# Opening loads, first-chunk normalisation, group-load timing and final-store queue of a one-core attention + gMLP kernel

## The chip, the cores and the metric

The kernel runs on one core of a Trainium2 chip. The metric is device time in microseconds (us) of one execution. Before the change the median of four runs is 1329.87 us (1329.43 to 1330.57).

A core has five engines that run their own instruction streams in order: TensorE (PE in the profile, with PEld for its weight loads), VectorE (DVE), ScalarE (ACT), GpSimd (POOL) and SyncE (SP). DMA transfers are issued by SP, ACT or POOL as instructions of their streams, so a DMA waits behind whatever its issuer is still waiting for; the transfer itself runs beside the engines. Matrix products land in PSUM banks; operands lie in SBUF.

## The reference, cut to what matters

One block with adaptive layer norms: a modulation vector from `c`, grouped-query attention (32 query heads, 8 key/value groups, 2048 tokens, 2048 cached keys, head size 128), and a gated MLP whose spatial product mixes tokens.

```python
mod = (silu(c) @ w_mod).reshape(1, 6, 1, 512)
sa, ca, ga, sb, cb, gb = mod[:, 0..5]
h = layernorm(x) * (1 + ca) + sa                    # x: 1 x 2048 x 512
q = h @ wq                                          # 32 heads of 128
o = softmax(q @ k_cache.T * 128**-0.5) @ v_cache    # 4 query heads per k/v group
x = x + ga * (o @ wo)
h = layernorm(x) * (1 + cb) + sb
z = gelu(h @ w_in);  z1, z2 = halves of z;  z2 = layernorm(z2)
x = x + gb * ((z1 * (w_sp @ z2 + b_sp)) @ w_out)
```

## The kernel before

Tokens are 16 tiles of 128 rows, taken in four chunks of four tiles (CT = 4). The attention runs as 128 units: unit `it` is group `it // 16`, token tile `it % 16`, all four query heads of the group. A unit has eight slots. In a slot, `qk` (L914) makes two score matmuls of 128 keys by 512 columns (4 heads x 128 rows) into a two-bank PSUM tile, and ACT takes the exponential of 1024 columns; `pv` (L936) makes eight matmuls of the previous unit's probabilities by the values, with normalisation by VectorE after every half of a unit (`rall`, `onorm`, L955 and L956), and after slot 7 a DMA transpose of the result (`oT`, L964, on SP). Three units later `wo_proj` (L968) multiplies by `wo`.

The order of all instructions is written out by hand. `at(it, slot, fn)` puts a piece of work ahead of the slot's score matmuls; `fill[it, slot]` lists matmuls that come after them. The loop at L1202 emits slot by slot; each engine keeps the order in which its instructions were emitted. `qproj(b, ...)` (L873) projects the queries of block b (one group, one chunk) as fill matmuls, with a copy of each PSUM bank to SBUF by VectorE (`qT`, L894).

Layer norm of a chunk has three pieces: `ln1_stats` (L796: two VectorE instructions per tile, then two small ones on POOL for the reciprocal root, `rstd_of` L669), `ln1_norm` (L801: one VectorE pass per tile), and the turn to columns with scale and shift. For chunk 0 and 1 the turn is on TensorE, `ln1_turn` (L824), through the two PSUM banks called `misc`, with `ln1_mod` (L814) out of PSUM by VectorE, or in part by ACT; for chunks 2 and 3 it is by DMA transposes on SP (`ln1_dma`, L852) and in-place `ln1_mod` passes (L857). The `misc` banks also hold the modulation columns, the query projections and the `wo` products.

The opening is issued on SP in this order: `c`, row tile 0 of x, the first third of `w_mod` (L698, columns for shift and scale), half the keys of group 0 in natural order, `wq` of group 0, row tiles 1 to 3 of x (L735), the other keys by DMA transpose, values, the rest of x, `wo`. TensorE fills the time with `warm(n)` matmuls on zeros (L762), then `mod_columns` (L774) makes the shift and scale columns; row tile 0 is normalised, turned and projected, and unit 0 begins. Row tiles 1 to 3 are normalised together (L904), turned at slot 4 of unit 0, and projected in slots 5 to 7.

Group g's keys (SP transpose), values, `wo` and `wq` (POOL queue) are loaded by four entries at L1109 to L1114. The rest of `w_mod` and `w_in` come on POOL at units 2 and 5.

After the attention, the second layer norm, `w_in` products with gelu (`z2`, `z1`), and the spatial product run (`spatial`, L1274, `gb` L1294); `finish_tile` (L1308) scales, adds the residual (`yout`, two buffers) and stores a row tile. Between the first and second quarter of the spatial product SP issues 16 transposing loads of the last quarter of `w_sp` (L1340 to L1342, `load_wsp` L1055).

Of the kernel before, what the change touches and what calls it, by code (L numbers as in the profile page):

```python
# [15 lines left out]
P = 128  # L16
# [559 lines left out]
def kernel(  # L576
# [19 lines left out]
    nc = tc.nc  # L596
    _, S, D = A_x.shape
    _, HKV, SK, DH = A_k_cache.shape
    HQ = A_wq.shape[1] // DH
    REP = HQ // HKV  # L600
# [4 lines left out]
    NT = S // P  # L605
# [4 lines left out]
    CT = 512 // P  # L610
# [7 lines left out]
    x_dram = A_x[0].rearrange("(t p) d -> p t d", p=P)  # L618
    out_dram = out[0].rearrange("(t p) d -> p t d", p=P)
# [6 lines left out]
    wmod_dram = w_mod.rearrange("(p dt) n -> p dt n", p=P)  # L626
    c_dram = c[0].rearrange("(p j) -> p j", p=P)
# [18 lines left out]
    x_sb = res.tile([P, NT, D], BF16, name="x_sb")  # L646
# [9 lines left out]
    wmod_a = res.tile([P, NDT, 2 * D], BF16, name="wmod_a")  # L656
# [6 lines left out]
    def bank(name):  # L663
        return psum.tile([P, 512], FP32, name=name)
# [28 lines left out]


    c_bf = res.tile([P, NDT], BF16, name="c_bf")
    nc.sync.dma_start(out=c_bf[:], in_=c_dram)
    nc.sync.dma_start(out=x_sb[:, 0, :], in_=x_dram[:, 0, :])
    nc.sync.dma_start(out=wmod_a[:], in_=wmod_dram[:, :, 0 : 2 * D])  # L698
    k_nat = early.tile([P, SK], BF16, name="kT")
    nc.sync.dma_start(out=k_nat[:, 0:HK].rearrange("p (t d) -> p t d", d=DH), in_=k_rows)  # L700

    groups, wqs, hTs, qTs = {}, {}, {}, {}

    def load_wq(g, engine):
        wqs[g] = early.tile([P, NDT, REP * DH], BF16, name="wq_g")
        engine.dma_start(
            out=wqs[g][:], in_=wq_dram[:, :, g * REP * DH : (g + 1) * REP * DH]
        )

    def load_v(g):  # L710
        v1 = late.tile([P, NKT, DV], BF16, name="v1")
        nc.gpsimd.memset(v1[:, :, DH:DV], 1.0)  # L712
        if g > 0:
            nc.gpsimd.dma_start(out=v1[:, :, 0:DH], in_=v_dram[:, g])
        else:
            nc.sync.dma_start(out=v1[:, 0 : NKT // 2, 0:DH], in_=v_rows)
            nc.sync.dma_start(
                out=v1[:, NKT // 2 : NKT, 0:DH], in_=v_dram[:, 0, NKT // 2 : NKT]
            )
        groups[g]["v1"] = v1  # L720

    def load_wo(g, engine):
        wo_g = late.tile([P, REP, D], BF16, name="wo_g")
        engine.dma_start(out=wo_g[:], in_=wo_dram[:, g * REP : (g + 1) * REP, :])
        groups[g]["wo"] = wo_g

    def load_k(g):
        kT = early.tile([P, SK], BF16, name="kT")
        nc.sync.dma_start_transpose(out=kT[:], in_=A_k_cache[0, g])
        groups[g] = dict(kT=kT)  # L730
# [31 lines left out]
    def warm(n):  # L762

        w_ps = bank("o_ps")
        for k in range(n):
            nc.tensor.matmul(
                w_ps[:].rearrange("p (r d) -> p r d", r=REP),
                lhsT=zeros[:, 0, :],
                rhs=zeros[:],
                start=True,  # L770
                stop=True,
            )
# [23 lines left out]
    def ln1_stats(j0, n):  # L796
        for j in range(j0, j0 + n):
            ln_stats(mv1, j, x_sb[:, j, :])
        return rstd_of(mv1[:, j0 : j0 + n, :], n, "ln1")

    def ln1_norm(j0, n, rstd):  # L801
        xns = []
        for j in range(j0, j0 + n):
            xn = res.tile([P, D], BF16, name="xn1", bufs=4)
            normalise(xn[:], x_sb[:, j, :], mv1[:, j, 0:1], rstd[:, j - j0 : j - j0 + 1])
            xns.append(xn)
        return xns

    def hT_of(ch):
        if ch not in hTs:  # L810
            hTs[ch] = res.tile([P, NDT, 512], BF16, name="hT", bufs=NCH)
        return hTs[ch]
# [11 lines left out]
    def ln1_turn(j0, n, xns, on_act=()):  # L824

        ch, c0 = j0 // CT, (j0 % CT) * P
        hT = hT_of(ch)
        for half in range(2):
            t_ps = bank("misc")[:].bitcast(BF16).rearrange("p (k q) -> p k q", k=2)
            for k in range(2):  # L830
                dt = half * 2 + k
                for jj in range(n):
                    nc.tensor.transpose(  # L833
                        t_ps[:, k, jj * P : (jj + 1) * P],
                        xns[jj][:, dt * P : (dt + 1) * P],
                        ident[:],
                    )
            for k in range(2):
                dt = half * 2 + k
                dst, src = hT[:, dt, c0 : c0 + n * P], t_ps[:, k, 0 : n * P]  # L840
                if dt in on_act:
                    nc.scalar.activation(
                        out=dst,
                        in_=src,
                        func=ACT.Identity,
                        scale=modc[:, NDT + dt : NDT + dt + 1],
                        bias=modc[:, dt : dt + 1],
                    )
                else:
                    ln1_mod(dst, src, dt)  # L850
# [7 lines left out]
        for dt in range(NDT):  # L858
            ln1_mod(hTs[ch][:, dt, :], hTs[ch][:, dt, :], dt)

    warm(18)
    xns0 = ln1_norm(0, 1, ln1_stats(0, 1))
    mod_columns(0, wmod_a, 0)
    ln1_turn(0, 1, xns0, on_act=(1, 3))
# [3 lines left out]
            k_ps[:, kt * P : (kt + 1) * P], k_nat[:, kt * P : (kt + 1) * P], ident[:]  # L868
        )
    nc.scalar.copy(out=kT0[:, 0:HK], in_=k_ps)  # L870
    warm(3)

    def qproj(b, heads, c0, n):  # L873

        g, ch = divmod(b, NCH)
        if b not in qTs:
            qTs[b] = early.tile([P, REP, 512], BF16, name="qT")
        one = n * len(heads) <= 512
        ps = {}

        def mm(hh, dt):
            if dt == 0 and (not one or hh == heads[0]):
                ps[0] = bank("misc")
            o0 = (hh - heads[0]) * n if one else 0
            nc.tensor.matmul(  # L885
                ps[0][:, o0 : o0 + n],
                lhsT=wqs[g][:, dt, hh * DH : (hh + 1) * DH],
                rhs=hTs[ch][:, dt, c0 : c0 + n],
                start=(dt == 0),
                stop=(dt == NDT - 1),  # L890
            )
            if dt == NDT - 1 and (not one or hh == heads[-1]):
                hs = heads if one else [hh]
                nc.vector.tensor_copy(  # L894
                    out=qTs[b][:, hs[0] : hs[-1] + 1, c0 : c0 + n],
                    in_=ps[0][:, 0 : len(hs) * n].rearrange("p (h q) -> p h q", q=n),
                )

        return [lambda hh=hh, dt=dt: mm(hh, dt) for hh in heads for dt in range(NDT)]

    for fn in qproj(0, list(range(REP)), 0, P):
        fn()
    rest0 = {}
    rest0["xn"] = ln1_norm(1, CT - 1, ln1_stats(1, CT - 1))  # L904


    NU = HKV * NT
# [3 lines left out]
    def at(it, slot, fn):  # L911
        later.setdefault((it, slot), []).append(fn)
# [148 lines left out]
    wsp = [None] * NCH  # L1061

    fill = {}
    rest_q = qproj(0, list(range(REP)), P, 512 - P)
    at(0, 4, lambda: ln1_turn(1, CT - 1, rest0["xn"]))
    for k, fn in enumerate(rest_q):
        fill.setdefault((0, 5 + k // 6), []).append(fn)
    for i in range(4):
        fill[0, i] = [lambda: warm(1)]

    def ln1_at(ch, stats, norm, turn):
        st = {}
        at(*stats, lambda: st.update(r=ln1_stats(ch * CT, CT)))
        at(*norm, lambda: st.update(x=ln1_norm(ch * CT, CT, st["r"])))
        if ch == 1:
            at(*turn, lambda: ln1_turn(ch * CT, CT, st["x"]))
        else:
            at(norm[0], norm[1] + 1, lambda: ln1_dma(ch * CT, CT, st["x"]))
            at(*turn, lambda: ln1_dma_mod(ch))

    ln1_at(1, (1, 0), (1, 5), (1, 7))
    ln1_at(2, (2, 4), (3, 1), (4, 5))
    ln1_at(3, (5, 1), (5, 5), (6, 6))
    rest_w = {}
    at(2, 5, lambda: nc.gpsimd.dma_start(out=wmod_b, in_=wmod_dram[:, :, 2 * D : NMOD]))
    at(5, 5, lambda: nc.gpsimd.dma_start(out=win_sb[:], in_=win_dram))
# [20 lines left out]
    for st in range(NT):  # L1107
        at(21 + 6 * st, 2, lambda st=st: load_wsp(wsp[0], 0, st))
    for g in range(1, HKV):  # L1109
        it = (g - 1) * NT + 4  # L1110
        at(it, 3, lambda g=g: load_k(g))
        at(it + 1, 3, lambda g=g: load_v(g))
        at(it + 2, 3, lambda g=g: load_wo(g, nc.gpsimd))
        at(it + 3, 3, lambda g=g: load_wq(g, nc.gpsimd))  # L1114


    zs = {}
# [127 lines left out]
    for f in range(NFT):  # L1245
# [6 lines left out]
        out=ok1[:], in0=rall[:], scalar1=1.0 / SAFE, scalar2=None, op0=ALU.is_ge  # L1252
# [8 lines left out]
        out=bad[:], in0=okm[:], scalar1=-1.0, scalar2=1.0, op0=ALU.mult, op1=ALU.add  # L1261
# [46 lines left out]
    def finish_tile(t, jj, src, parts=1):  # L1308
        j = t * CT + jj
        tmp = mlp.tile([P, D], FP32, name="tmp", bufs=2)  # L1310
        yout = mlp.tile([P, D], BF16, name="yout", bufs=2)
        w = D // parts
        for k in range(parts):
            s = slice(k * w, (k + 1) * w)
            nc.vector.tensor_tensor(out=tmp[:, s], in0=src[:, s], in1=gb_rows[:, s], op=ALU.mult)
            nc.vector.tensor_tensor(out=yout[:, s], in0=tmp[:, s], in1=x_sb[:, j, s], op=ALU.add)
            (nc.sync, nc.scalar)[k].dma_start(out=out_dram[:, j, s], in_=yout[:, s])

    yTs = {}

# [81 lines left out]
```

## Time and profile before

| what | value |
|---|---|
| median of runs | 1329.87 us |
| profiled execution | 1329.66 us |
| its span, first to last instruction | 1327.8 us |
| TensorE busy | 1314.4 us (99%) |
| ACT busy | 1078.0 us (81%) |
| VectorE busy | 473.2 us (36%) |
| first score matmul | 11.76 us |
| last unit's score matmuls end, last matmul of the kernel | about 1138 and 1321 us |
| granted TensorE clock, mean | 0.999 |

In a row of the timeline the first number is the start in us from the span's start, the second the duration (of merged rows: of the whole stretch), then the engine, the line of the kernel, the operation, output and inputs, count, and in brackets how long the engine stood idle before it and what released it. `SPq` and `ACTq` are DMA issues in those engines' streams; the duration is that of the issue, not of the transfer. In the waits view a row gives who waited for whom, and the total in us, the number of times and the longest.

### The profile page before, as it was taken

The numbers are of one execution on the slowest core, as the hardware profiler recorded it, in microseconds if no ns is written. First come the engines' busy times: TensorE is split into PE (matmuls) and PEld (weight loads), VectorE is DVE, ScalarE is ACT, GpSimd is POOL, SyncE is SP. The second block draws the span as 40 slices with busy tenths as digits, with TensorE's granted clock in tenths as the row PEclk, the third lists the DMA queues.
The fourth block names the chain that finished last, engine by engine and source line by source line (L and its number), as shares of the span: only waits on it lengthen the run. The fifth ranks groups of instructions, "written<-read, shape, count | busy, mean of one in ns | idle before, by whom it ended". The sixth has DMA issues, their size and how long they took to land.

```text
span 1327.8 us, 27856 instructions
## 1 busy us (share of the span) xinstructions
PE 1314.4 (99%) x12337; PEld 858.7 (65%) x12337; DVE 473.2 (36%) x1163; ACT 1078.0 (81%) x1060; POOL 48.5 (4%) x90
## 2 busy tenths in 40 slices
PE   8999999999999999999999999999999999999998
PEld 5666666666666666666666666666666666644445
DVE  5632222222222222222222222222222566793444
ACT  6888999999999999999999999999999999650000
POOL 1200000000000000000000000000000000120000
PEclk9999999999999999999999999999999999999999
DMA  5541031003201131013100410122101111153300
GB/s 160 118 129 13 17 70 31 17 17 67 35 17 21 33 69 21 13 37 68 18 18 17 84 21 15 21 65 36 21 13 21 25 34 33 29 119 80 64 21 27
DMA packets 145983, 57.58 MB, mean 43 GB/s; under 512 B 136160, under 2 KB 141408, under 8 KB 145856
## 3 DMA queue, kind: packets, MB, share of 16 engines
q1 hardware_dynamic: 141504, 39.29, 15.6%
q0 software_dynamic: 4208, 16.39, 4.4%
q8 instruction: 98, 1.61, 0.5%
q14 instruction: 29, 0.24, 0.1%
q10 hardware_dynamic: 144, 0.07, 0.0%
HBM read 21.37 MB, written 2.10 MB: 18 GB/s over the span
## 4 chain that ended last, share of the span: by engine, by line
PE 96%; SPq 2%; DMA 1%; DVE 1%; issue 0%; POOL 0%; DVEq 0%
PE o_ps L944 35%; PE s_ps L922 33%; PE misc L976 8%; PE misc L885 8%; PE misc L1279 6%; PE s_ps L1125 2%; PE s_ps L1164 2%; SPq L1056 1%; PE o_ps L1300 1%; PE s_ps L1300 1%; DMA wmod_a<-in_w_mod_dram 0%; DMA hT<-xn 0%; DMA out_dram<-yout 0%; PE misc L833 0%; DVE qT L894 0%
## 5 line engine op out<-in xcount | busy, mean ns | idle before, releaser
L929 ACT ACTIVATE pT<-s_ps 128x1024 bf16<-128x1024 f32 x1024 | 1044.5, 1025 | 86.9 <-PE s_ps L922 13.0
L944 PEld LDWEIGHTS <-pT 128*128 128x128 bf16 x8192 | 548.5, 98 | 242.4 <-issue 1.3
L944 PE MATMUL o_ps<-v,pT 128*128 128x129 bf16 x8192 | 631.4, 220 | 1.0 <-DVE onorm L956 1.0
L922 PE MATMUL s_ps<-qT,kT 128*128 128x512 bf16 x2048 | 608.9, 379 | 1.8 <-DVE qT L894 1.4
L955 DVE RECIPROCAL rall<-o_ps 128x2 f32<-128x2 f32 x256 | 43.7, 171 | 737.7 <-PE o_ps L944 737.4
L922 PEld LDWEIGHTS <-kT 128*128 128x128 bf16 x2048 | 199.2, 98 | 121.4 <-issue 1.7
L976 PE MATMUL misc<-wo_g,oT 128*128 128x512 bf16 x512 | 194.0, 379 | 0.0
L885 PE MATMUL misc<-hT,wq_g 128*128 128x512 bf16 (+2 forms) x528 | 190.3, 373 | 0.0
L956 DVE TENSOR_TENSOR onorm<-o_ps,rall 128x256 bf16<-128x256 f32 x256 | 108.6, 424 | 9.0 <-DVE rall L955 0.3
L1279 PE MATMUL misc<-wsp,z 128*128 128x512 bf16 (+2 forms) x560 | 100.7, 336 | 1.5 <-DVE gb L1294 1.5
L894 DVE CAST qT<-misc 128x512 bf16<-128x512 f32 (+1 forms) x129 | 87.3, 677 | 6.7 <-PE misc L885 6.6
L1279 PEld LDWEIGHTS <-z 128*128 128x128 bf16 x560 | 50.7, 98 | 50.0 <-issue 1.5
L989 DVE TENSOR_TENSOR xacc<-misc,xacc 128x512 f32<-128x512 f32 x112 | 76.2, 680 | 0.0
L885 PEld LDWEIGHTS <-wq_g 128*128 128x128 bf16 x528 | 50.6, 98 | 1.8 <-issue 0.3
L976 PEld LDWEIGHTS <-oT 128*128 128x128 bf16 x512 | 50.1, 98 | 0.7
L1294 DVE TENSOR_TENSOR gb<-misc,bsp_bc 128x512 bf16<-128x512 f32 (+1 forms) x28 | 18.4, 658 | 53.2 <-PE misc L1279 53.2
L712 POOL MEMSET v<- 128x128 bf16 x8 | 1.6, 203 | 707.9 <-issue 606.9
L1125 PE MATMUL s_ps<-win_sb,hT 128*128 128x448 bf16 x128 | 27.0, 352 | 0.0
L1135 ACT ACTIVATE z<-s_ps 128x896 bf16<-128x896 f32 x16 | 14.7, 917 | 14.9 <-PE s_ps L1125 14.9
L1164 PE MATMUL s_ps<-hT,win_sb 128*128 128x512 bf16 x112 | 24.5, 379 | 0.0
L1172 ACT ACTIVATE z1T<-s_ps 128x1024 bf16<-128x1024 f32 x14 | 14.3, 1024 | 10.1 <-PE s_ps L1164 9.1
L691 DVE BATCH_NORM_STATS2 bnst<-x_sb 128x6 f32<-128x512 bf16 x32 | 21.8, 681 | 0.5
(78 smaller groups left out, 285.3 us busy)
## 6 DMA issues: line engine op xcount, KB each, us to landing
v<-in_A_v_cache_dram POOLq DMA_DIRECT2D x7, 512.0 KB, 7.1
wo_g<-in_A_wo_dram POOLq DMA_DIRECT2D x7, 512.0 KB, 4.7
wq_g<-in_A_wq_dram POOLq DMA_DIRECT2D x7, 512.0 KB, 5.9
oT<-onorm SPq DMA_TRANSPOSE x128, 2.4
wsp<-in_w_mod_dram POOLq DMA_DIRECT2D x1, 2048.0 KB, 10.1
out_dram<-yout SPq DMA_DIRECT2D x15, 128.0 KB, 1.7
win_sb<-in_B_w_in_dram POOLq DMA_DIRECT2D x1, 1792.0 KB, 10.5
x_sb<-in_A_x_dram SPq DMA_DIRECT2D x3, 512.0 KB, 6.3
```

Source lines behind the costliest of these rows:

```text
L885: nc.tensor.matmul(ps[0][:, o0 : o0 + n], lhsT=wqs[g][:, dt, hh * DH : (hh + 1) * DH], rhs=hTs[ch][:, dt, c0 : c0 + n], start=(dt == 0), s ...
L894: nc.vector.tensor_copy(out=qTs[b][:, hs[0] : hs[-1] + 1, c0 : c0 + n], in_=ps[0][:, 0 : len(hs) * n].rearrange("p (h q) -> p h q", q=n),)
L922: nc.tensor.matmul(s_ps[:, h * 512 : (h + 1) * 512].rearrange("p (r q) -> p r q", r=REP), lhsT=groups[g]["kT"][:, kt * P : (kt + 1) * P], ...
L929: nc.scalar.activation(out=pTs[u][:, 2 * i : 2 * i + 2, :], in_=s_ps[:].rearrange("p (k q) -> p k q", k=2), func=ACT.Exp, scale=inv_sqrt_dh,)
L944: nc.tensor.matmul(o_ps[:, hh % 2, 0 : DH + 1], lhsT=pTs[u][:, kt, hh * P : (hh + 1) * P], rhs=groups[g]["v1"][:, kt, 0 : DH + 1], start=( ...
L955: nc.vector.reciprocal(out=rall[:, c0 : c0 + 2], in_=o_ps[:, :, DH])
L956: nc.vector.tensor_tensor(out=onorms[u][:, hh - 1 : hh + 1, :], in0=o_ps[:, :, 0:DH], in1=rall[:, c0 : c0 + 2].unsqueeze(2).to_broadcast([ ...
L976: nc.tensor.matmul(X_ps[:], lhsT=oTs[u][:, hh, :], rhs=groups[g]["wo"][:, hh, :], start=(hh == 0), stop=(hh == REP - 1),)
L989: nc.vector.tensor_tensor(out=xaccs[j][:], in0=X_ps[:], in1=xaccs[j][:], op=ALU.add)
L1125: nc.tensor.matmul(ps[0][:, hf * 512 : hf * 512 + FC], lhsT=h2Ts[j // CT][:, dt, (j % CT) * P : (j % CT + 1) * P], rhs=win_sb[:, dt, FH + ...
L1164: nc.tensor.matmul(ps[0][:, k * 512 : (k + 1) * 512], lhsT=win_sb[:, dt, f * P : (f + 1) * P], rhs=h2Ts[2 * ch2 + k][:, dt, :], start=(dt ...
L1279: nc.tensor.matmul(g_ps[:, :n], lhsT=z2[:, st, f * P : (f + 1) * P], rhs=wsp[t][:, st, c0 : c0 + n], start=(st == 0), stop=(st == NT - 1 a ...
```

## The change

Five edits:

1. `c` and row tile 0 are issued on ACT's queue; SP starts with `w_mod`, in two loads of 512 columns each.
2. The warm-up matmuls go from 18 and 3 to 14 and 2, and those in unit 0 from four to two.
3. Row tiles 1 to 3 of chunk 0 are handled in two steps, row tile 1 and then 2 and 3. The statistics of tile 1 are emitted before the first query projection, its turn at unit 0 slot 1, its projection (128 columns of all heads) in slot 3; tiles 2 and 3 are turned at slot 4 and projected (256 columns, two heads per bank) in slots 6, 7 and slot 0 of unit 1. The first projection's copy is shared by VectorE and ACT.
4. Chunk 1's statistics move from unit 1 slot 0 to slot 1; chunk 3's scale and shift from unit 6 slot 6 to unit 7 slot 4. The loads of each next group move from units 4 to 7 of the group's sixteen to units 7 to 9.
5. `finish_tile` stores on ACT's queue (the second half of the last tile on SP).

```diff
-    nc.sync.dma_start(out=c_bf[:], in_=c_dram)
-    nc.sync.dma_start(out=x_sb[:, 0, :], in_=x_dram[:, 0, :])
-    nc.sync.dma_start(out=wmod_a[:], in_=wmod_dram[:, :, 0 : 2 * D])
+    nc.scalar.dma_start(out=c_bf[:], in_=c_dram)
+    nc.scalar.dma_start(out=x_sb[:, 0, :], in_=x_dram[:, 0, :])
+    for i in range(2):
+        part = slice(i * D, (i + 1) * D)
+        nc.sync.dma_start(out=wmod_a[:, :, part], in_=wmod_dram[:, :, part])
...
-    warm(18)
+    warm(14)
...
-    warm(3)
-
-    def qproj(b, heads, c0, n):
+    warm(2)
+    first = {}
+    first["r1"] = ln1_stats(1, 1)
+
+    def qproj(b, heads, c0, n, two_engines=False):
...
-                nc.vector.tensor_copy(
-                    out=qTs[b][:, hs[0] : hs[-1] + 1, c0 : c0 + n],
-                    in_=ps[0][:, 0 : len(hs) * n].rearrange("p (h q) -> p h q", q=n),
-                )
+                dst = qTs[b][:, hs[0] : hs[-1] + 1, c0 : c0 + n]
+                src = ps[0][:, 0 : len(hs) * n].rearrange("p (h q) -> p h q", q=n)
+                cut = len(hs) // 2 if two_engines else len(hs)
+                nc.vector.tensor_copy(out=dst[:, 0:cut], in_=src[:, 0:cut])
+                if two_engines:
+                    nc.scalar.copy(out=dst[:, cut:], in_=src[:, cut:])
...
-    for fn in qproj(0, list(range(REP)), 0, P):
+    for fn in qproj(0, list(range(REP)), 0, P, two_engines=True):
         fn()
-    rest0 = {}
-    rest0["xn"] = ln1_norm(1, CT - 1, ln1_stats(1, CT - 1))
+    first["x1"] = ln1_norm(1, 1, first["r1"])
+    first["r2"] = ln1_stats(2, 2)
...
-    rest_q = qproj(0, list(range(REP)), P, 512 - P)
-    at(0, 4, lambda: ln1_turn(1, CT - 1, rest0["xn"]))
-    for k, fn in enumerate(rest_q):
-        fill.setdefault((0, 5 + k // 6), []).append(fn)
-    for i in range(4):
-        fill[0, i] = [lambda: warm(1)]
+    def first_turn():
+        ln1_turn(1, 1, first["x1"])
+        first["x2"] = ln1_norm(2, 2, first["r2"])
+
+    at(0, 1, first_turn)
+    at(0, 4, lambda: ln1_turn(2, 2, first["x2"]))
+    fill[0, 0] = [lambda: warm(1)]
+    fill[0, 2] = [lambda: warm(1)]
+    fill[0, 3] = qproj(0, list(range(REP)), P, P)
+    rest_q = qproj(0, [0, 1], 2 * P, 2 * P) + qproj(0, [2, 3], 2 * P, 2 * P)
+    fill[0, 6], fill[0, 7], fill[1, 0] = rest_q[0:4], rest_q[4:10], rest_q[10:16]
...
-    ln1_at(1, (1, 0), (1, 5), (1, 7))
+    ln1_at(1, (1, 1), (1, 5), (1, 7))
     ln1_at(2, (2, 4), (3, 1), (4, 5))
-    ln1_at(3, (5, 1), (5, 5), (6, 6))
+    ln1_at(3, (5, 1), (5, 5), (7, 4))
...
-        it = (g - 1) * NT + 4
-        at(it, 3, lambda g=g: load_k(g))
-        at(it + 1, 3, lambda g=g: load_v(g))
-        at(it + 2, 3, lambda g=g: load_wo(g, nc.gpsimd))
-        at(it + 3, 3, lambda g=g: load_wq(g, nc.gpsimd))
+        it = (g - 1) * NT
+        at(it + 7, 6, lambda g=g: load_k(g))
+        at(it + 8, 3, lambda g=g: load_v(g))
+        at(it + 9, 3, lambda g=g: load_wo(g, nc.gpsimd))
+        at(it + 7, 3, lambda g=g: load_wq(g, nc.gpsimd))
...
-            (nc.sync, nc.scalar)[k].dma_start(out=out_dram[:, j, s], in_=yout[:, s])
+            (nc.scalar, nc.sync)[k].dma_start(out=out_dram[:, j, s], in_=yout[:, s])
```

## The prediction

> **What bounds the kernel now.** I read the page first, then the waits of TensorE, then the timeline of the three places where TensorE waits.
>
> ```profile
> PE 1314.4 (99%) x12337; PEld 858.7 (65%) x12337; DVE 473.2 (36%) x1163; ACT 1078.0 (81%) x1060; POOL 48.5 (4%) x90
> ```
>
> TensorE is busy for 99% of the span. Any time it does not stand idle is already useful work, so a change that removes no useful matmul can only win or lose at its few stalls. Two rows of the timeline tell how regular the middle is: the first score matmuls of units 16 and 17 start at 158.57 and 167.38, 8.81 us apart. The loads of group 2 onwards, at either place, fall into such stretches. The waits of TensorE name the stalls:
>
> ```profile
> PE misc L1279 <- DVE gb L1294: 1.5, 1, 1.5
> ...
> PE o_ps L944 <- DVE onorm L956: 1.0, 1, 1.0
> ```
>
> The 1.5 is near the end (1244 us), the 1.0 at 80 us; the six others (4.1 us together) lie in the first 23 us. The timeline of the opening (columns: start, duration, engine, line, operation):
>
> ```profile
> 1.64 0.69 SPq L698 DMA_DIRECT2D wmod_a<-in_w_mod_dram  x1
> ...
> 3.50 0.82 SPq L735 DMA_DIRECT2D x_sb<-in_A_x_dram  x1
> ...
> 11.02 0.69 DVE L894 CAST qT<-misc 128x512 bf16<-128x512 f32 x1 [1.64 <-PE misc L885]
> ...
> 22.47 0.60 PE L922 MATMUL s_ps<-qT,kT 128*128 128x512 bf16 x2 [0.65 <-DVE qT L894]
> ...
> 27.09 1.38 DVE L680 TENSOR_SCALAR xn<-x_sb,mv,rstd_ln 128x512 bf16<-128x512 bf16 x4 [0.24 <-POOL rstd_ln L676]
> ```
>
> The last of these rows is a deadline: chunk 1's normalised rows are complete at 28.47 (27.09 + 1.38), and the timeline has TensorE's transposes of them start at 28.68, with 0.2 us to spare. Chunk 1's statistics had begun at 22.33, as soon as VectorE was through with the last copy of unit 0's queries. Then the two later stalls:
>
> ```profile
> 79.50 1.38 DVE L815 TENSOR_SCALAR hT<-hT,modc 128x512 bf16<-128x512 bf16 x4 [7.24 <-DMA hT<-xn]
> ...
> 81.48 0.61 PE L944 MATMUL o_ps<-v,pT 128*128 128x129 bf16 x8 [1.02 <-DVE onorm L956]
> ...
> 1220.65 21.41 SPq L1056 DMA_TRANSPOSE wsp<-in_B_w_sp_dram  x16
> ...
> 1242.16 5.47 SPq L1317 DMA_DIRECT2D out_dram<-yout  x4
> ...
> 1244.18 0.69 DVE L1316 TENSOR_TENSOR yout<-tmp,x_sb 128x512 bf16<-128x512 f32 x1 [7.94 <-DMA out_dram<-yout]
> ...
> 1245.53 10.52 PE L1279 MATMUL misc<-wsp,z 128*128 128x512 bf16 x48 [1.50 <-DVE gb L1294]
> ```
>
> At 80 us VectorE sits for 7.24 us on chunk 3's DMA transposes, and everything queued behind it starves TensorE. At 1242 us four stores leave SP only when its 16 weight transposes are issued.
>
> **Final stores on ACT's queue.** VectorE's third output tile needs one of two yout buffers; the first store is issued at 1242.16 although its tile was ready at 1227.04. On ACT's queue nothing stands ahead (its last gelu ends at 1197.5), so that store goes out about 15 us earlier; median landing is 1.7 us and tiles come 4.96 us apart. VectorE's 7.94 us wait and TensorE's 1.50 go; next late is nothing, since 0.69 + 0.69 of output work fits in 4.96. Gain 1.5. Were the stores slowed by the 16 transposes beside them, a buffer is free for two tiles, 9.9 us, so only a landing above that brings a stall back. At the very end the halves of the last tile change queues: SP's half landed in 2.4 us, ACT's in 1.9, so the last store costs between -0.2 and +0.5 us; I take 0, because the issues (0.33 and 0.38) are nearly equal.
>
> **Loads and chunk 3 later.** Chunk 3's scale-and-shift moves from unit 6, slot 6 to unit 7, slot 4. Unit 7 lasts 10.13 us (75.46 to 85.59) where 8.81 is the pitch with the same matmuls: the stall costs 1.32. The new place is TensorE's 79.86, and the transposes landed by 79.50 even with 3.3 MB of group loads beside them; with k, v, wo and wq of group 1 moved to units 7 to 9 only win (1.8 MB) shares their stretch, so they land sooner. Chunk 3's queries are projected from unit 8; four passes of 0.41 us end in time. Gain 1.32, bounds 1.0 and 1.32. What is moved: per group one SP transposing load (issue 2.48, ahead of SP's oT transposes, whose results are wanted 1.5 units, 13 us, later) and three POOL issues of 0.75 to 1.23 on an engine 4% busy. They arrive 4 or more units before use. Cost 0; without that cover, the 2.48 on SP.
>
> **Opening loads.** SP issues w_mod at 0.73 instead of 1.64, 0.91 earlier. Two parts read 1 KB rows where one load read 2 KB: by the windows view the DMA moves 392 GB/s in 6 to 7 us (2 KB rows) and 372 in 8 to 9 (1 KB), so 1 MB costs 0.15 more. The 128 KB row tile, sent ahead before, now rides beside w_mod: 0 to 0.35 at 372 GB/s. The DMA is full from 4 to 10.7 us, so all that follows comes 0.4 to 0.75 earlier; I take 0.6. Rows 1-3 of x landed at 10.70 (3.50 plus 7.2), now 10.1; wq at 9.6, now 9.0.
> The Trainium skill, DMA: Bandwidth & Descriptors, section Issuing engines are not separate DMA queues, says that DMAs started by different engines share the same 16 DMA engines and that a second queue saves only the starter's issue time. By it alone x would land 0.91 earlier and the total below would be 0.3 us lower; the sum stays with the rows.
> The new c and x issues on ACT come either ahead of the activation-table load (0.73, 1.28 us) or behind it, 1.28 later. Row 0 would then be normalised at about 7.3 instead of 6.0; both are hidden, because the first projection waits for wq until 9.0 and VectorE for x until 10.1. Price 0 either way. Seven warm-up matmuls fewer (25 to 18) free 7 x 0.216 = 1.5 us of TensorE that lay in waits: 0.
>
> **Two-step normalisation.** Here I follow VectorE's order. Behind row 0's scale-and-shift it now holds the statistics of row 1, and these wait for x at 10.1: two instructions, 0.90 us (11.62 to 12.52), end 11.0. The query copy is behind them, halved: rows give 0.69 for 512 columns and 0.56 for 384, so 0.43 for 256, end 11.4; ACT's half is long done. First scores at 11.45, before 11.76: 0.3 won. Row 1: POOL chain 1.02 (4.56 to 5.58), so normalised 12.0 to 12.4. Rows 2's and 3's statistics: 1.7, to 14.1. Row 1's four scale-and-shifts: 4 x 0.31, to 15.3. Rows 2-3 normalised 2 x 0.38, to 16.05. TensorE meanwhile does the projection of slot 3, which waits for 15.3: 13 matmuls of 0.066 more, to 16.2; its copy (0.69) ends at 16.95. The second half of the next transposes needs that PSUM bank (misc has two), so slot 4's scores start at 17.3, before 17.13. The early win is gone. From there ACT leads: exponentials every 0.92, slot 7's scores at 19.9, six matmuls, unit 1 at 20.95 (before 22.47), its second fill of six ends at 22.5, where slot 1 starts; before 23.36. That is 0.9 won.
> But chunk 1's statistics moved behind the copy of that second fill: 22.5 + 0.69 = 23.2, before 22.33. Statistics 3.28, POOL chain 1.48 (25.61 to 27.09), normalising 1.38: complete at 29.3. TensorE arrives for the transposes 5.32 after slot 1 (as 23.36 to 28.68), at 27.8; twelve of 16 need the last row, so they end at 30.05, before 29.57. The head loses 0.5. Bounds: 0.9 won if the statistics chain does not bind, 1.3 lost if x lands at 10.7 as now and 0.2 more slips.
>
> **Sum.** -1.5 - 1.32 + 0.5 = -2.3 us on the profiled execution, which took 1329.66 us (span 1327.8 plus 1.9 around it), 0.2 under the median 1329.87. From the median: 1327.6. A measurement of this kernel can tell about 0.2%, 2.7 us; this lies just inside.
>
> **Rivals.**
> The chain of chunk 1 does not bind: some 1.5 us shorter (x rows earlier, shorter copies, or statistics running between other work). For it: VectorE had 1.64 us idle before 11.02 and 0.24 at 27.09. Against: its order is fixed and POOL's 1.48 stands in it. Then the head wins 0.9: 1329.87 - 3.7 = 1326.2.
> One removed stall stays: chunk 3's mods still wait, or the stores crawl beside the 16 transposes (21.41 us of SP). Against: 79.50 is already early enough, and the DMA share is 0.31 at 1243 to 1247. Then 1328.9 to 1329.1.
> The head costs more: x rows land 1 to 2 us later than I take, because ACT's queue or the SP issues push them. Time 1328.6 to 1329.6.
> Slower than before: one mechanism, VectorE's statistics of row 1 standing ahead of the query copy. Every microsecond of x beyond 10.1 delays first scores, and the whole chain to 30 us, one to one. It equals the 2.3 won at a landing of 12.4, and from 15.1 the kernel is slower by 0.2%, 1332.6. Against: the transfers ahead of x are the same bytes and x landed at 10.70.
>
> **How the numbers follow.** Forecast 0.48 (own range 1327.0 to 1328.4; a quarter of it under 1327.2, the 0.2% mark), chain not binding 0.27, one stall stays 0.12, dearer head 0.09, slower 0.04. Faster: 0.27 + 0.12 = 0.39. Same: 0.36 + 0.21 = 0.57. Slower 0.04. The range takes in the second case with 0.3 below it and the dearer cases: 1325.9 to 1329.6.
>
> **What would show it.** Right: no wait of TensorE on gb at 1244; unit 7 at 8.81; row 1's statistics starting just as x lands near 10.1; first scores near 11.45; slot 1 of unit 1 near 22.5 and then a stall of 1 to 1.5 us on xn before unit 1's last slot, its scores near 30.05. Wrong: no stall there, statistics of row 1 starting before 9.5 or after 11, or a new wait of ACT's stores.

## The result

The changed kernel takes 1328.48 us (median; 1327.98 to 1329.61), the kernel before 1329.71 us over its runs on the same chips. The ratio is 0.999, with a 95% interval of 0.9985 to 0.9995: a gain of 1.2 us, clear of zero by the interval and well under the 0.2% mark. The forecast was 1327.6, a gain of 2.3. The profiled execution took 1328.36 us, with a span of 1326.6 us, 1.2 less than before.

Where the time went is read by setting the starts of the same matmuls of the two traces beside each other:

| point of the trace | before | after | difference so far |
|---|---|---|---|
| first score matmul | 11.76 | 11.99 | +0.23 |
| unit 1, slot 1 | 23.36 | 22.44 | -0.92 |
| unit 1, slot 7 | 29.63 | 30.19 | +0.56 |
| unit 16, slot 0 | 158.57 | 157.81 | -0.76 |
| last matmul | 1321.05 | 1318.73 | -2.32 |
| issue of the last store | 1323.19 | 1320.86 | -2.33 |
| end of the span | 1327.8 | 1326.6 | -1.2 |

(The prediction, and an expectation below, have 29.57 for slot 7 of unit 1 in the kernel before. That is the start of the slot's weight load; its score matmuls start at 29.63.)

So TensorE was ahead by the forecast 2.3 us when it finished, and 1.1 us of it was given back after the last store, where the prediction had put 0.

The five longest waits of TensorE in the changed kernel (the opening's initial 1.2 is as before):

```profile
PE s_ps L928 <- ACT qT L903: 1.7, 1, 1.7
PE o_ps L768 <- DVE onorm L750: 1.2, 1, 1.2
PE s_ps L928 <- ACT pT L935: 0.8, 2, 0.7
PE misc L784 <- DMA wmod_a<-in_w_mod_dram: 0.6, 1, 0.6
PE misc L835 <- DVE xn L680: 0.5, 1, 0.5
```

The 1.5 on gb and the 1.0 on onorm are gone. New are the first line, first scores held by ACT's half of the query copy, and the last, chunk 1's transposes held by the normalised rows. The timeline of the opening shows both; first the same transposes and scores in the kernel before:

```profile
28.73 1.06 PE L833 MATMUL misc<-ident,xn 128*128 128x128 bf16 x16
29.63 0.59 PE L922 MATMUL s_ps<-qT,kT 128*128 128x512 bf16 x2
```

and then the changed kernel:

```profile
10.31 0.69 DVE L691 BATCH_NORM_STATS2 bnst<-x_sb 128x6 f32<-128x512 bf16 x1 [1.69 <-DMA x_sb<-in_A_x_dram]
...
11.14 0.39 DVE L901 CAST qT<-misc 128x256 bf16<-128x256 f32 x1
...
11.57 0.37 ACT L903 CAST qT<-misc 128x256 bf16<-128x256 f32 x1 [1.47 <-DVE qT L901]
...
23.25 0.68 DVE L691 BATCH_NORM_STATS2 bnst<-x_sb 128x6 f32<-128x512 bf16 x1
...
28.02 1.38 DVE L680 TENSOR_SCALAR xn<-x_sb,mv,rstd_ln 128x512 bf16<-128x512 bf16 x4 [0.97 <-POOL rstd_ln L676]
...
28.48 1.87 PE L835 MATMUL misc<-ident,xn 128*128 128x128 bf16 x16 [0.55 <-DVE xn L680]
...
30.19 0.59 PE L928 MATMUL s_ps<-qT,kT 128*128 128x512 bf16 x2
```

VectorE stands 1.69 us for the rows of x, ACT's half starts only behind VectorE's half (11.57 after 11.14 + 0.39), chunk 1's statistics begin at 23.25 where they had begun at 22.33, and the 16 transposes take 1.87 us where they took 1.06 before, because their rows trickle in.

The rows for the two later stalls:

```profile
81.56 1.37 DVE L817 TENSOR_SCALAR hT<-hT,modc 128x512 bf16<-128x512 bf16 x4
...
1231.71 9.83 ACTq L1328 DMA_DIRECT2D out_dram<-yout  x4
...
1243.21 0.69 DVE L1305 TENSOR_TENSOR gb<-misc,bsp_bc 128x512 bf16<-128x512 f32 x1 [2.03 <-PE misc L1290]
...
1320.86 0.37 SPq L1328 DMA_DIRECT2D out_dram<-yout  x1
```

Chunk 3's scale and shift runs without a wait, unit 7 takes 8.81 us, and VectorE waits for TensorE at 1243 instead of for a store.

### The profile page after: what moved, and what is told of

Its sections match the earlier page's. It is cut to its first block, busy times and chain, and to the rows that moved or that the text cites. A ratio compares the mean times of both kernels' runs of the same rounds, so it can differ in the third digit from the quotient of the medians.

```text
span 1326.6 us, 27888 instructions
## 1 busy us (share of the span) xinstructions
PE 1313.1 (99%) x12346; PEld 859.0 (65%) x12346; DVE 473.3 (36%) x1166; ACT 1078.2 (81%) x1061; POOL 49.2 (4%) x92
## 4 chain that ended last, share of the span: by engine, by line
PE 98%; DVE 1%; DMA 1%; ACT 0%; SPq 0%; POOL 0%; issue 0%
PE o_ps L950 35%; PE s_ps L928 33%; PE misc L982 8%; PE misc L889 8%; PE misc L1290 7%; PE s_ps L1136 2%; PE s_ps L1175 2%; PE o_ps L1311 1%; DMA x_sb<-in_A_x_dram 1%; PE s_ps L1311 1%; DVE bnst L691 0%; ACT pT L935 0%; PE misc L1052 0%; DVE qT L901 0%; DVE xn L680 0%; SPq L700 0%
## 5 line engine op out<-in xcount | busy, mean ns | idle before, releaser
L1183 ACT ACTIVATE z1T<-s_ps 128x1024 bf16<-128x1024 f32 x14 | 14.3, 1024 | 10.1 <-PE s_ps L1175 9.1
L708 POOL DMA_DIRECT2D wq_g<-in_A_wq_dram x7 | 5.3, 750 | 420.9 <-PE misc L889 420.9
```

## The experiments

The profiled kernels differ by a few tenths in when the first rows of x land (row 1's statistics start at 10.09 to 10.79 in the kernels with the new opening, the first scores at 11.76 to 12.09 in those with the old one). Readings below are therefore taken inside one trace, from one point to another, and the span is given beside them.

**The end: final stores alone.** Theory: the last store on SP delays SP's way out of the redo check. Rival: the store's landing was late by chance.

```diff
-            (nc.sync, nc.scalar)[k].dma_start(out=out_dram[:, j, s], in_=yout[:, s])
+            (nc.scalar, nc.sync)[k].dma_start(out=out_dram[:, j, s], in_=yout[:, s])
```

> The kernel before with edit 5 alone (all stores on ACT's queue, the very last half on SP). Theory: TensorE's 1.50 us wait on gb at 1244 goes, so the last matmul comes 1.5 earlier (1321.05 to 1319.55), but the end after the last store's issue grows from 4.6 to 5.7 us, because SP now issues that store and only then branches out of the redo check: its next instruction comes about 3.0 us after the branch, and then its 1.4 us row of semaphore steps ends the kernel. Net -0.4: span 1327.4. Rival (the end cost is the landing of the store in the changed kernel's one profile, chance): the end stays at 4.6 and the span is 1326.3.

Measured: span 1327.1 (1329.01 us, ratio 0.9995, interval 0.9986 to 1.0004). The wait on gb is gone. From the last store's issue at 1321.51 to the last step is 5.52 us, against 4.59 in the kernel before. Edit 5 wins 1.5 and gives 0.9 back.

**The end: only the very last half back on ACT.**

```diff
-            (nc.scalar, nc.sync)[k].dma_start(out=out_dram[:, j, s], in_=yout[:, s])
+            ((nc.scalar, nc.sync) if parts == 1 else (nc.sync, nc.scalar))[k].dma_start(...)
```

> The changed kernel with the two halves of the very last tile on the queues of the kernel before (first half SP, second ACT). Theory (SP's exit is late because SP issues the last store): the last store's issue stays at 1320.86 and the end follows 4.6 us later as in the kernel before, span 1325.5, 1.1 less than the changed kernel. SP's first step after its branch comes 2.7 to 3.0 us after the branch, whatever has landed. Rival (the landing of the last 64 KB decides): the end moves with the landing time only, and a landing of 2.7 us on ACT's queue would leave the span at 1326.6.

Measured: span 1325.7, 1327.68 us, ratio to the kernel before 0.9984 (0.9975 to 0.9993). From the last store's issue to the end 4.52 us, although the opening was 0.3 slower. The issues of its last tile, then the issue of the last store in the kernel before (on ACT), and the wait of SP after its branch in the changed kernel and then here (the waits view of SP; who waited, for whom, total, times, longest):

```profile
1320.37 0.37 SPq L1328 DMA_DIRECT2D out_dram<-yout  x1
...
1321.17 0.34 ACTq L1328 DMA_DIRECT2D out_dram<-yout  x1
```

```profile
1323.19 0.38 ACTq L1317 DMA_DIRECT2D out_dram<-yout  x1
```

```profile
SPq L1378 <- SPq L1378: 3.0, 1, 3.0
```

```profile
SPq L1378 <- SPq L1378: 2.6, 1, 2.6
```

At the end of the kernel every engine branches past the redo path, which does not run here. After that branch SP, ACT and VectorE each do nothing for 2.5 to 3.2 us (POOL, which branches some 75 us earlier, goes on after 0.18). In the instruction records of the kernel before and the changed kernel, SP's branch at 1322.77 (before) is followed by its next step at 1325.48, and at 1321.29 (after) by 1324.32; ACT's at 1324.15 by 1326.87, and at 1321.00 by 1323.90; VectorE's, which issues no store, at 1323.45 by 1326.51. The store in the changed kernel was issued at 1320.86 and landed 2.7 us later, at 1323.6; SP came back 0.7 after that. So the landing did not hold the end. What comes after differs by engine: from SP's return to the last step are 2.2 us (a row of some 20 semaphore steps), from ACT's 0.9. An engine that issues the last store branches behind it: ACT 0.96 us after its issue (the load of the flag stands between), SP 0.43. That gives 0.43 + 3.03 + 2.2 = 5.66 on SP (5.66 measured) and 0.96 + 2.72 + 0.91 = 4.59 on ACT (4.59 measured). In the kernel before the two exits were nearly level: the last step of SP's row stood 0.1 us for ACT.

The Trainium skill, Runtime: NRT & Kernel Launch, section Instruction fetch mechanics, says that a taken branch to a target outside the fetched pages waits for a DMA fetch of the page. The 2.5 to 3.2 us behind a branch whose own record is 0.05 to 0.07 us agree with that; no run here moves the branch target, so the fetch itself is not shown, and why POOL needs only 0.18 stays open.

**The opening alone.** Edits 1 to 3 and the later place of chunk 1's statistics on the kernel before; that is the change without these lines:

```diff
-    ln1_at(3, (5, 1), (5, 5), (6, 6))
+    ln1_at(3, (5, 1), (5, 5), (7, 4))
...
-        it = (g - 1) * NT + 4
+        it = (g - 1) * NT
...
-            (nc.sync, nc.scalar)[k].dma_start(out=out_dram[:, j, s], in_=yout[:, s])
+            (nc.scalar, nc.sync)[k].dma_start(out=out_dram[:, j, s], in_=yout[:, s])
```

> The kernel before with edits 1 to 3 and chunk 1's statistics in slot 1 (edits 4's other parts and 5 undone). Theory: the opening costs 0.6 us: unit 1's slot 7 scores at 30.19 where the kernel before has 29.57, nothing later changes, span 1328.4. Rival (the opening wins, and something later, made by the moved loads or stores, gives it back): slot 7 scores before 29.6 and a span under 1327.8.

Measured: span 1327.8, 1330.36 us, ratio 1.0006 (0.9997 to 1.0015). Slot 7's scores come at 30.09 (expected 30.19), 0.5 later than in the kernel before, but unit 16 starts at 158.60, as before (158.57): unit 7 takes 9.69 instead of 10.13. Its timeline says why:

```profile
79.54 1.38 DVE L817 TENSOR_SCALAR hT<-hT,modc 128x512 bf16<-128x512 bf16 x4 [6.80 <-DMA hT<-xn]
```

Chunk 3's transposes land at 79.5, as in the kernel before, so a TensorE that is 0.5 late finds a stall that is 0.4 shorter. The opening's loss is real but hidden there, and it shows in full only when the chunk 3 stall is removed. The costs of edits 1 to 4 are not additive.

**Chunk 1's statistics back to slot 0**, on the changed kernel.

```diff
-    ln1_at(1, (1, 1), (1, 5), (1, 7))
+    ln1_at(1, (1, 0), (1, 5), (1, 7))
```

> The changed kernel with chunk 1's statistics back in slot 0 of unit 1, ahead of the second query copy on VectorE. Theory (VectorE's order makes TensorE's stall at chunk 1's transposes): statistics begin at about 21.6 instead of 23.25, normalised rows are complete at 27.8 instead of 29.40, the stall of 1.2 us at the transposes goes and unit 1's slot 7 scores come at 28.8 instead of 30.19: span 1325.3, 1.3 less. The query copy then ends near 25.5, in time for unit 2. Rival (the stall is set by POOL or by the free PSUM banks): the copy, now 3.3 us later, holds its misc bank and the stall moves to the second half of the transposes; span 1326.3 or more.

Measured: span 1325.4, 1327.18 us, ratio to the kernel before 0.9979 (0.997 to 0.9988). From its timeline:

```profile
21.95 0.68 DVE L691 BATCH_NORM_STATS2 bnst<-x_sb 128x6 f32<-128x512 bf16 x1
...
25.15 0.66 DVE L901 CAST qT<-misc 128x512 bf16<-128x512 f32 x1
...
26.72 1.39 DVE L680 TENSOR_SCALAR xn<-x_sb,mv,rstd_ln 128x512 bf16<-128x512 bf16 x4 [0.34 <-POOL rstd_ln L676]
...
28.23 1.06 PE L835 MATMUL misc<-ident,xn 128*128 128x128 bf16 x16
...
29.13 0.59 PE L928 MATMUL s_ps<-qT,kT 128*128 128x512 bf16 x2
```

The transposes run in 1.06 us without a wait, and the query copy at 25.15 disturbs nobody. From unit 1's slot 1 to slot 7 it is 6.23 us here (22.90 to 29.13), 7.75 in the changed kernel and 6.26 in the kernel before. One slot number costs 1.5 us.

**The first query copy on ACT alone**, on the changed kernel.

```diff
-                cut = len(hs) // 2 if two_engines else len(hs)
-                nc.vector.tensor_copy(out=dst[:, 0:cut], in_=src[:, 0:cut])
                 if two_engines:
-                    nc.scalar.copy(out=dst[:, cut:], in_=src[:, cut:])
+                    nc.scalar.copy(out=dst, in_=src)
+                else:
+                    nc.vector.tensor_copy(out=dst, in_=src)
```

> The changed kernel with the first projection's copy all on ACT, so that it is behind neither VectorE's wait for x nor VectorE's half. Theory (what follows in unit 0 hangs on VectorE's chain of row 1, rows 2-3 and two query copies, not on the first scores): first scores about 0.9 earlier, at 11.1, but slot 4's scores and unit 1's slot 1 within 0.3 of 17.2 and 22.44 and a span within 0.4 of 1326.6. Rival (first scores set the opening, as the prediction's one-to-one rule of x has it): slot 1 at 21.6 and a span of 1325.7.

Measured: span 1326.7, 1328.55 us. TensorE's rows:

```profile
11.22 0.59 PE L928 MATMUL s_ps<-qT,kT 128*128 128x512 bf16 x2 [0.67 <-ACT qT L901]
...
17.40 1.02 PE L928 MATMUL s_ps<-qT,kT 128*128 128x512 bf16 x4
...
22.64 0.59 PE L928 MATMUL s_ps<-qT,kT 128*128 128x512 bf16 x2
```

First scores come 0.8 earlier, slot 4's and unit 1's are not earlier at all (17.40 and 22.64 against 17.20 and 22.44, with x 0.2 later). The first scores are not on the path that sets the opening; VectorE's chain from row 1's statistics on is.

**Chunk 3's later place alone**, on the kernel before.

```diff
-    ln1_at(3, (5, 1), (5, 5), (6, 6))
+    ln1_at(3, (5, 1), (5, 5), (7, 4))
```

> The kernel before with chunk 3's scale and shift moved to unit 7 slot 4 and nothing else. Theory (the later place alone removes the stall, since the transposes have landed by then): unit 7 takes 8.81 instead of 10.13 us, VectorE waits for no hT transposes, span 1326.5. Rival (the moved group loads are needed too): transposes still under way at slot 4, unit 7 at 9.2 us or more.

Measured: unit 7 takes 8.81, VectorE has no wait for the transposes; span 1327.3 with an opening 0.3 later than in the kernel before and 0.4 more on the gb wait (1.9); 1328.96 us, ratio 0.9993 (0.9984 to 1.0002). The span expected was 1326.5; the stall behaved as expected, and the 0.3 and the 0.4, in places that this edit does not touch, make up the rest.

**The group loads' later place alone**, on the kernel before (four entries, of which the first lines).

```diff
-        it = (g - 1) * NT + 4
-        at(it, 3, lambda g=g: load_k(g))
+        it = (g - 1) * NT
+        at(it + 7, 6, lambda g=g: load_k(g))
...
```

> The kernel before with the group loads moved and chunk 3 left at unit 6 slot 6. The prediction's view: with only w_in beside them the transposes of chunk 3 land sooner, before 77.8, so VectorE's 7.24 us wait shrinks below 5.6 and unit 7 comes down to 8.8 to 9.0. Rival, from the changed kernel, where SP took 11.1 us to issue the four transposes with the group loads gone, as before: the group loads don't matter, the transposes land near 79.5, unit 7 stays at 10.0 to 10.2, span 1327.8.

Measured: span 1328.0, 1329.80 us, ratio 0.9995 (0.9986 to 1.0004). VectorE's row and SP's:

```profile
79.27 1.38 DVE L815 TENSOR_SCALAR hT<-hT,modc 128x512 bf16<-128x512 bf16 x4 [6.67 <-DMA hT<-xn]
```

```profile
64.07 10.34 SPq L855 DMA_TRANSPOSE hT<-xn  x4
```

The transposes land at 79.3 instead of 79.5, and SP still needs 10.3 us to issue the four (11.06 before, 11.13 in the changed kernel). Unit 7 comes to 9.56, below the rival's 10.0, but 0.3 of that is the later opening, as in the run of the opening alone.

The run does not test what it was made for, because the loads did not move away. POOL's rows in the kernel before and then here:

```profile
62.96 1.23 POOL L714 DMA_DIRECT2D v<-in_A_v_cache_dram  x1
...
64.95 0.75 POOL L724 DMA_DIRECT2D wo_g<-in_A_wo_dram  x1
65.69 0.75 POOL L706 DMA_DIRECT2D wq_g<-in_A_wq_dram  x1
```

```profile
63.96 0.76 POOL L706 DMA_DIRECT2D wq_g<-in_A_wq_dram  x1
...
64.93 1.16 POOL L714 DMA_DIRECT2D v<-in_A_v_cache_dram  x1
66.08 0.76 POOL L724 DMA_DIRECT2D wo_g<-in_A_wo_dram  x1
```

The entries at units 7 to 9 set only the order of POOL's instructions. Nothing held group 1's three loads, so POOL issued them in unit 5, right behind w_in and beside the transposes, in this run as in the changed kernel (64.19 to 66.32). Only the keys, which SP issues, went later (51.75 to 82.50), and before they had landed at 56.5, ahead of the transposes. So the two readings differ by 0.2 us in kernels that put the same 3.3 MB of POOL loads beside the transposes; what the transposes would do without them was not tried.

**Three edits together** (x8 in the texts below): the last half on ACT, chunk 1's statistics in slot 0, the first copy on ACT.

> The changed kernel with three edits: the last tile's second half on ACT's queue, chunk 1's statistics back in slot 0 of unit 1, and the first query copy all on ACT. Theory: the first two add up, 1.06 at the end and 1.3 to 1.5 in the opening, and the third is worth 0 to 0.2 now that chunk 1's statistics no longer set the opening: span 1324.0, about 2.6 under the changed kernel and 3.8 under the kernel before, median near 1325.9. Rival (they share a cause or one hides the other): a span of 1325.0 or more.

Measured: span 1324.0, 1326.15 us, ratio to the kernel before 0.9971 (0.996 to 0.9982). The gains add up: 2.6 us of span under the changed kernel, of which 1.5 lie between slots 1 and 7 of unit 1 (6.23 against 7.75) and 1.2 behind the last store (4.50 against 5.66).

**The redo flag loaded early** (x9), on top of that, and then **no store on SP at all**.

```diff
+    redo = nc.values_load(flag[0:1, 0:1], min_val=0, max_val=P)
     finish_tile(last, CT - 1, o2_last[CT - 1], parts=2)
...
-    redo = nc.values_load(flag[0:1, 0:1], min_val=0, max_val=P)
```

> The kernel of x8 with the engines' loads of the redo flag ahead of the last tile's work instead of behind its stores. Theory (the end is the branch of the engine that leaves last plus about 2.9 us): ACT's branch comes 0.43 instead of 0.96 us after it issues the last store, but SP, whose branch is 0.4 us before that store and whose 1.4 us of semaphore steps follow, then sets the end: 0.2 to 0.3 us less than x8, span 1323.8. Rival (landing of the stores sets the end): no change against x8.

Measured: span 1324.1, 1325.99 us; no gain. ACT's branch did come at 0.37 us after its store, but SP's return took 3.14 us after its branch (2.68 in the three-edit kernel) and ended the kernel 4.97 us behind the last store. That SP would set the end was expected, the gain of 0.2 to 0.3 was not met.

```diff
-            ((nc.scalar, nc.sync) if parts == 1 else (nc.sync, nc.scalar))[k].dma_start(...)
+            nc.scalar.dma_start(out=out_dram[:, j, s], in_=yout[:, s])
```

> The kernel of x9 with both halves of the last tile on ACT's queue, so that SP issues no output store at all and branches long before the end. Theory (the end is set by the exit of the engine that leaves last): SP is waiting at its steps already, ACT branches 0.4 us after the last store, resumes 2.6 to 2.9 us later, and the kernel ends about 1.0 us after that: 4.1 us from the last store's issue to the end, where x8 has 4.50 and x9 4.97; a span of 1323.6 at the same opening as x8. Rival (SP's branch is not what made x9's end late, the landing of the last halves is): 4.5 us or more.

Measured: span 1324.5, 1326.06 us, 4.59 us from the last store's issue to the end, where 4.1 was expected. From its timeline:

```profile
1319.02 1.83 ACTq L1328 DMA_DIRECT2D out_dram<-yout  x2
```

The second of two stores in a row on ACT took 1.04 us to issue instead of 0.34, so ACT branched 1.07 us after it; 2.61 us later ACT was back and 0.91 after that the kernel ended. By its number alone the run falls to the rival (4.5 or more). The trace speaks against it: the last store's counter had released SP 1.4 us before ACT was back, so it was ACT's exit and not the landing that ended the kernel, and the 4.1 was missed by the longer issue. The three versions end within 0.2 us of each other by their medians, and the measurement doesn't tell them apart; the three-edit kernel is the simplest of them.

## Why the prediction was right, and where it was off

- Final stores, gain 1.5: right, the wait on gb went. The reason held with less room than said. "On ACT's queue nothing stands ahead" was wrong: the first store was to leave at once, and it left at 1231.71, 5.4 us after its tile was ready at 1226.28, 10.5 us earlier than before and not 15. That is the "new wait of ACT's stores" which the prediction had named as a sign of being wrong; it cost nothing. In the instruction list each store waits for one of eight DMA counters that SP's loads use as well, and so for an earlier load of the 16. The third tile's output, at 1235.52, still found its buffer free.
- The end, cost -0.2 to +0.5, taken as 0: this is the step that failed. It was "the last store costs between -0.2 and +0.5 us; I take 0, because the issues (0.33 and 0.38) are nearly equal". It cost 1.07 in the profile (5.66 against 4.59). Landings and issues were the wrong rows to bound it with; what counts is when the issuing engine reaches its branch and what it has still to do behind it. The branch records are in the trace of before, and its last 4.6 us behind the last store were in view. Why an engine stands still behind that branch stays open.
- Chunk 3, gain 1.32: right, by the later place alone. "They land sooner" was wrong, and so was its reason, that only w_in would share their stretch: POOL issued group 1's v, wo and wq at 62.96 to 65.69 before and at 64.19 to 66.32 in the changed kernel. The last transpose landed at 80.25, later than before (79.42); the new place (81.56) had a margin of 1.3 us all the same. What held is the step's other half, that the place is late enough.
- Opening, loss of 0.5: right in size (0.56) and in place. Unit 1's slot 1 was forecast at 22.5 and came at 22.44, statistics at 23.2 and came at 23.25, rows complete at 29.3 and came at 29.40, slot 7 at 30.05 and came at 30.19. Rows 1 to 3 landed at 10.29 (3.27 + 7.02) where 10.1 was forecast. "First scores at 11.45" was wrong by 0.54, mostly because the halves of the copy ran one after the other (0.39 and 0.37 us against 0.69 for one copy): the instruction list has ACT's half wait for VectorE. The rest is the later x. "The whole chain one to one" with x holds for VectorE's chain; the run with the copy on ACT shows that it doesn't hold through the first scores.
- The Trainium skill, DMA: Bandwidth & Descriptors, section Issuing engines are not separate DMA queues, taken alone, would have put x 0.91 us earlier; the traces have 0.36 (landed at 10.65 before, 10.29 after). That is less than the issue time, which the page gives as all that a second queue can save; the change also split w_mod and moved the row tile beside it, and no run here takes these apart.
- Rivals: none of them happened. Chunk 1's chain did bind, no removed stall stayed, x came 0.2 later than forecast and not 1 to 2. The time lies 0.1 above the forecast case's own range, by the exit, which was no rival at all.

By its own sum: -1.5 - 1.32 + 0.5 against -1.5 (and 0.06 more behind unit 16) - 1.32 + 0.56 + 1.07, which is the -1.2 of the span.

## What to carry to other kernels

Treat the exit as a stage of its own: on each engine follow the records from its last DMA issue through the last branch to the final semaphores, and put the last store on the engine that has least to do behind it. When a step is split or moved by one slot on an engine that is mostly idle, write down that engine's order of instructions; here one slot (1.5 us) was worth more than everything else in the opening. A place in the program on an engine that waits for nothing is an order and not a time: POOL issued in unit 5 what was written into units 7 to 9, so look for the issue in the trace before counting on the move. And before adding up gains, ask whether a stall is fixed in absolute time, as by a DMA landing: a loss ahead of it then costs nothing until someone removes the stall.

## What the runs showed of the hardware that was not expected

- 2.5 to 3.2 us pass between an engine's branch past the redo path at the end and its next instruction, on SP, ACT and VectorE alike, in all twelve traces (in the run without a store on SP, SP branches 75 us earlier and then waits for landings). On POOL it is 0.18 us in all of them.
- The third of chunk 3's four DMA transposes of 128 x 512 took 6.3 to 7.0 us to issue on SP in all twelve traces, where the other three took 1.2 to 1.6. In all of them POOL's loads of w_in, v, wo and wq (3.3 MB) were issued beside these transposes; whether they are the cause was not tried.
- Two 64 KB stores issued 0.8 us apart on ACT's queue took 0.34 and 1.04 us to issue in one trace; alternating between SP and ACT each takes 0.33 to 0.38. Nearness alone is not the reason: in the changed kernel two 128 KB stores 0.45 us apart on ACT (1236.48 and 1236.93) took 0.35 and 0.39.
- The activation-table load sat behind ACT's two DMA issues (at 1.62 us, where it had been at 0.73), which the prediction had left open; it cost nothing. The Trainium skill, ScalarE: Activation LUTs, section Step-by-step: what each stage is for, has the compiler place it right before the first function that needs it, and the trace agrees (1.62 + 1.28, the first ACTIVATE at 2.91).
